# Gate steps reordered around the ReLU, and the gated activation written over it in one ring of four

## Chip, cores and metric

The kernel runs on one core of a Trainium2 chip. The metric is the device time of one execution, in microseconds (us); lower is better. Three executions of the kernel before gave a median of 2806.07 us.

## What is computed

A long convolution with a gate, then two wide two-matmul layers, all in float32. The part that matters here is the gate and the two layers behind it:

```python
y = np.fft.irfft(Uf * Hf[None, :, :], n=L, axis=1)[:, :S, :]
x = (x * y).reshape(B * S, D)          # the gate; B*S = 24960 tokens, D = 128
h = x @ w_in                           # 2048 hidden columns
x = (h * np.clip(h + 3.0, 0.0, 6.0) / 6.0) @ w_out
h = np.maximum(x @ w_in2, 0.0)
out = (h * h) @ w_out2
```

## The kernel before, in words

The first 465 us or so make the convolution's spectrum. The rest, the expert stage, is what the change touches. Its tokens come in 64 groups `j` of 390 (one `s4(j)` gives one group of the convolution's result) and are worked on in 49 tiles `t`: the first of 390 tokens, the others of up to 512. A tile can take tokens of one group or two; a group that lies across two tiles is rounded in two pieces.

The order of the work is written out by hand: `tiles` is a list of (layer, tile), and each entry has eight steps, of 256 hidden columns each. The first 15 tiles of layer 0 stand alone (early tiles); from then on tiles of layer 0 and of layer 1 alternate (the interleaved part), and at the end layer 1 is alone. Within a step `n`, the instructions are issued in this order, and each engine runs its own in the order issued:

- `l1(n)`: six matmuls into a PSUM tile `ph` (a ring of three), from the rounded input and its remainder. Matmuls need both as float32r: `oh`/`ol` in layer 0, `xh`/`xl` in layer 1 (high part, low part).
- `l2(n-3)`: six matmuls into the tile's sum `acc`. The first two need only the high part `gh` of an activation with the low weights, the last two the low part `gl`.
- `early_do[n]`: what the plan puts ahead of the ReLU.
- `relu(n)` on ScalarE into `r` (L618 in layer 0, L620 in layer 1), then `act(n)` on VectorE, which multiplies `r` with `ph` into `g` (L629, L632).
- `split(n-1)`: `gh` on ScalarE (L639, rounding), then `gl = g - gh` (L643), on VectorE or on GpSimd by the step's place in its tile. From step 112 on, even places are VectorE's, odd ones GpSimd's.
- `late_do[n]`: what the plan puts behind that, among it `combine(j)` (L500, sums of spectra for `s4`) and loads.
- one or two pieces of the decoding of the other weights (L104 to L127), whose last piece runs at 807.6 us.

`r` and `g` are rings of two each, so `act(n)` waits until `gl(n-2)` has read the `g` that it overwrites.

The gate of a group `j`: `s4(j)` is spread over a step or more between the matmuls of `l1` and `l2` and writes PSUM tile `py` (L517). VectorE multiplies it with the loaded `xt` in place (L532), ScalarE rounds it to `oh` (L534), VectorE subtracts to `ol` (L540). `py` lies in one of two banks that it shares with the sums `acc`: the bank is handed on to a tile's `acc` only when `ol` is done. For a tile that needs two groups, the first group's `s4` runs in the first one or two steps `8i`, `8i+1` of the tile before it in the list, and its bank is that of this tile's own `acc`, whose first matmul stands at step `8i+3`. On an early tile (`rate` 2) the product is planned at `8i+1` and `ol` at `8i+2`, in the interleaved part (`rate` 1) both at `8i+2`.

Of the kernel before, what the change touches and what calls it, by code (L numbers as in the profile page):

```python
# [7 lines left out]
F32 = mybir.dt.float32  # L8
F32R = mybir.dt.float32r
U32 = mybir.dt.uint32  # L10
AF = mybir.ActivationFunctionType
ALU = mybir.AluOpType
# [19 lines left out]
TM = 512  # L32
# [11 lines left out]
def tile_hyena_moe(ctx: ExitStack, tc, xg, vg, xT, pos, w1d, w2d, fmat, fwin, twc,  # L44
                   tws, twcf, twsf, dcs, inv, vtab, w_in1, w_out1, w_in2, w_out2, out):
    nc = tc.nc
# [234 lines left out]
    with tc.tile_pool(name="mlp", bufs=2, side="right") as mp, \  # L281
# [40 lines left out]
        for c in range(16):  # L322
# [10 lines left out]
            for q in range(4):  # L333
                ov = hs[q][:N1].rearrange("p d (h a) -> p a h d", h=2)
                src = fps[:N1, :, :, 32 * q:32 * q + 32]
# [32 lines left out]
    def idle(ps, count):  # L368
        for _ in range(count):
            nc.tensor.matmul(ps[:, 0, :TOK], wh[0][:, 0, :128], wh[0][:, 0, :TOK])  # L370
# [4 lines left out]
    with tc.tile_pool(name="cv_ps", bufs=4, space=PSUM) as vps:  # L375
# [17 lines left out]
        for i in range(NI + 2):  # L393
# [25 lines left out]
            for t, f in ((a + 6, load), (a + 3, product)):  # L419
                g, s = divmod(t, 3)  # L420
# [24 lines left out]
    mo = ctx.enter_context(tc.tile_pool(name="moe", bufs=2))  # L445
# [3 lines left out]
    def inputs(t):  # L449
        if (0, t) not in xin:  # L450
            xin[(0, t)] = tuple(mo.tile([128, TM], F32R, name=f"o{p}{t}", tag=f"o{p}", bufs=3)
                                for p in "hl")
        return xin[(0, t)]
# [50 lines left out]
    py = {}  # L504
# [19 lines left out]
    def ranges(j):  # L524
        for t in range(NTI):
            lo, hi = max(TOK * j, begins[t]), min(TOK * j + TOK, ends[t])
            if lo < hi:
                yield t, slice(lo - TOK * j, hi - TOK * j), slice(lo - begins[t], hi - begins[t])

    def gate(j):  # L530
        ps = py[j]
        nc.vector.tensor_tensor(ps[:, :TOK], ps[:, :TOK], xt.pop(j), ALU.mult)  # L532
        for t, src, dst in ranges(j):
            nc.scalar.activation(inputs(t)[0][:, dst], ps[:, src], AF.Copy)  # L534

    def gate_rest(j):
        ps = py.pop(j)
        for t, src, dst in ranges(j):
            h, l = xin[(0, t)]
            nc.vector.tensor_tensor(l[:, dst], ps[:, src], h[:, dst].bitcast(F32),  # L540
                                    ALU.subtract)

    begun, early_do, late_do = {}, {}, {}

    def plan(table, n, f, *args):
        table.setdefault(n, []).append((f, args))
# [7 lines left out]
    for t in range(1, NTI):  # L554
        js = list(range(last[t - 1] + 1, last[t] + 1))
        i = place_of[(0, t - 1)]
        n0, fast = NP * i, place_of[(0, t)] == i + 1
        if t == 1:
            jobs = [(js[0], 2, 2, i + 1), (js[1], 4, 2, i + 1)]
        else:  # L560
            jobs = [(js[-1], 4, 2 if fast else 0, i + 1)]
            if len(js) > 1:
                jobs.insert(0, (js[0], 0, 2 if fast else 1, i))
        assert len(js) == len(jobs)
        for j, q, rate, k in jobs:
            n = n0 + q
            plan(begun, n, s4, j, k)
            begun[n][-1] += (rate,)
            done = n + (4, 2, 1)[rate]
            gated[j] = done  # L570
            plan(early_do, done, gate, j)
            plan(early_do, done + (rate != 1), gate_rest, j)
            if j < 3:
                lead = (2, 1)
            elif j < 4:
                lead = (6, 5)
            else:
                lead = (7, 5)
            for back in lead:
                plan(late_do, n - back, combining, j)  # L580
            if j == 3:
                plan(late_do, 0, loads, j)
            elif j > 3:
                plan(late_do, gated[j - 3] + 1, loads, j)
# [12 lines left out]
    ph, rs, gs, gh, acc = ({} for _ in range(5))  # L597
# [15 lines left out]

    def relu(n):
        w = size[steps[n][1]]
        r = mo.tile([128, 2, TM], F32, name=f"r{n}", tag="r", bufs=2)
        if steps[n][0] == 0:
            nc.scalar.activation(r[:, :, :w], ph[n][:, :, :w], AF.Relu, bias=three)  # L618
        else:
            nc.scalar.activation(r[:, :, :w], ph[n][:, :, :w], AF.Relu)  # L620
        rs[n] = r

    def act(n):
        w = size[steps[n][1]]
        r, pv = rs.pop(n)[:, :, :w], ph.pop(n)[:, :, :w]
        gt = mo.tile([128, 2, TM], F32, name=f"g{n}", tag="g", bufs=2)
        g = gt[:, :, :w]
        if steps[n][0] == 0:
            nc.vector.scalar_tensor_tensor(g, r, 6.0, pv, ALU.min, ALU.mult)  # L629
        else:  # L630

            nc.vector.scalar_tensor_tensor(g, pv, 0.0, r, ALU.max, ALU.mult)  # L632
        gs[n] = g

    def split(n):
# [64 lines left out]
    decode(2, 1)  # L700
    decode(0, 3)
    gate(0)
    gate_rest(0)
    idle(mps.tile([128, 2, 512], F32, name="idle1", tag="ph", bufs=3), 6)
    decode(1, 3)
    decode(2, 6)
# [14 lines left out]
    for n in range(len(steps) + LAG + 1):  # L721
        if n < len(steps):
            l, j, q = steps[n]
            l1(n)
        m = n - LAG
        if 0 <= m < len(steps):
            l2(m)
        if 0 <= m - 1 < len(steps) and steps[m - 1][2] == NP - 1:
            finish(*steps[m - 1][:2])
        for f, args in early_do.pop(n, ()):  # L730
            f(*args)
        if n < len(steps):
            if q == 6 and n + 2 < len(steps) and steps[n + 2][0] == 1:
                part1(steps[n + 2][1])
            relu(n)
            act(n)
        if 0 <= n - 1 < len(steps):
            split(n - 1)
        for f, args in late_do.pop(n, ()):
            f(*args)  # L740
        for _ in range(2 if n < 14 else 1):
            next(rest, None)
# [94 lines left out]
```

## Time and profile before

| | before |
|---|---|
| median of three runs | 2806.07 us (2804.76 to 2806.34) |
| profiled execution, its own time | 2803.87 us |
| its span, first to last instruction | 2801.7 us |
| TensorE matmul (PE) busy | 2742.1 us, 98% |
| VectorE (DVE) busy | 1994.6 us, 71% |
| ScalarE (ACT) busy | 1931.6 us, 69% |
| GpSimd (POOL) busy | 1508.3 us, 54% |

Busy time is the time in which an engine has an instruction running. PE is the engine that has almost none to spare over the whole span; what the others do matters only where PE waits for them. The granted clock is the share of TensorE's full 2.4 GHz that it was given in a stretch: 0.5 is its lower level of 1.2 GHz. An idle time in a row is that of the engine just before the instruction, with what ended it.

### The profile page before, as it was taken

How to read it: one execution, taken by the hardware profiler on the slowest of the kernel's cores; microseconds unless marked ns; L12 is line 12 of the kernel's file. 1: busy time of each engine (PE TensorE's matmuls, PEld its weight loads, DVE VectorE, ACT ScalarE, POOL GpSimd, SP SyncE). 2: the span in 40 equal slices, each digit the busy share in tenths (PEclk: the TensorE clock that was granted, in tenths of full speed). 3: DMA queues.
4: the chain of work that ended last, by engine and by line, in shares of the span. 5: the costliest groups of instructions: out<-in, count | busy, mean ns of one | idle time of the engine just before them, and what ended most of it. 6: DMA issues, size and time to landing. Idle time of an engine off the chain costs nothing.

```text
span 2801.7 us, 34821 instructions
## 1 busy us (share of the span) xinstructions
PE 2742.1 (98%) x12862; PEld 2282.0 (81%) x12862; DVE 1994.6 (71%) x1976; ACT 1931.6 (69%) x2192; POOL 1508.3 (54%) x884
## 2 busy tenths in 40 slices
PE   7999998999999999999999999999999999999999
PEld 5899997777778888888888888888888888888887
DVE  6899998887876666666666666666666666666666
ACT  5445545666667777777777777777777777777776
POOL 3888884466565454444444444444545454444444
PEclk9999999999999999999999999999999999999999
DMA  3253535212111001010101010010101010000000
GB/s 120 85 165 109 149 112 123 79 31 71 40 32 34 25 18 35 18 35 18 35 18 35 19 35 19 25 29 25 29 25 29 25 29 4 8 8 12 12 12 16
DMA packets 136472, 122.35 MB, mean 44 GB/s; under 512 B 99370, under 2 KB 114798, under 8 KB 134894
## 3 DMA queue, kind: packets, MB, share of 16 engines
q1 hardware_dynamic: 127570, 86.27, 11.3%
q10 hardware_dynamic: 8732, 33.85, 4.4%
q8 instruction: 101, 1.65, 0.2%
q14 instruction: 69, 0.57, 0.1%
HBM read 83.68 MB, written 36.37 MB: 43 GB/s over the span
## 4 chain that ended last, share of the span: by engine, by line
PE 85%; DVE 6%; issue 3%; POOL 1%; ACT 1%; DMA 0%; POOLq 0%; DVEq 0%; ACTq 0%
PE acc L660 35%; PE ph L610 35%; PE p L225 7%; PE p L179 4%; PE py L517 3%; PE p L256 2%; DVE g L629 2%; DVE gl L643 1%; POOL gl L643 1%; ACT r L618 1%; ACT gh L639 0%; DVE wp L127 0%; DVE wa L114 0%; DVE py L532 0%; DVE a L198 0%
## 5 line engine op out<-in xcount | busy, mean ns | idle before, releaser
L643 POOL TENSOR_TENSOR gl<-g,gh 128x1024 fp32r<-128x1024 f32 (+2 forms) x401 | 970.7, 2421 | 1152.6 <-ACT gh L639 1101.0
L660 PE MATMUL acc<-gh,wp 128*128 128x512 f32 (+2 forms) x3136 | 878.7, 400 | 10.0 <-DVE ol L540 10.0
L639 ACT ACTIVATE gh<-g 128x1024 fp32r<-128x1024 f32 (+2 forms) x784 | 823.8, 1051 | 62.5 <-DVE g L629 36.2
L632 DVE SCALAR_TENSOR_TENSOR g<-ph,r 128x1024 f32<-128x1024 f32 (+2 forms) x392 | 477.9, 1219 | 363.6 <-POOL gl L643 268.1
L629 DVE SCALAR_TENSOR_TENSOR g<-r,ph 128x1024 f32<-128x1024 f32 (+2 forms) x392 | 475.9, 1214 | 361.9 <-POOL gl L643 276.5
L660 PEld LDWEIGHTS acc<-gh,wp 128*128 128x128 f32 x3136 | 577.9, 189 | 126.0 <-ACT gh L639 4.6
L618 ACT ACTIVATE r<-ph,three 128x1024 f32<-128x1024 f32 (+2 forms) x392 | 436.2, 1113 | 237.0 <-PE ph L610 232.4
L610 PE MATMUL ph<-oh,wp 128*128 128x512 f32 (+2 forms) x1568 | 573.3, 402 | 0.1
L610 PE MATMUL ph<-xh,wp 128*128 128x512 f32 (+2 forms) x1568 | 552.2, 393 | 0.0
L620 ACT ACTIVATE r<-ph 128x1024 f32<-128x1024 f32 (+2 forms) x392 | 401.8, 1025 | 177.2 <-PE ph L610 176.8
L660 PE MATMUL acc<-gl,wp 128*128 128x512 f32 (+2 forms) x1568 | 494.1, 396 | 8.6 <-POOL gl L643 8.1
L643 DVE TENSOR_TENSOR gl<-g,gh 128x1024 fp32r<-128x1024 f32 (+1 forms) x383 | 473.7, 1237 | 0.0
L660 PEld LDWEIGHTS acc<-gl,wp 128*128 128x128 f32 x1568 | 293.8, 189 | 83.3 <-POOL gl L643 14.8
L610 PEld LDWEIGHTS ph<-xh,wp 128*128 128x128 f32 x1568 | 294.4, 188 | 64.2
L610 PEld LDWEIGHTS ph<-oh,wp 128*128 128x128 f32 x1568 | 296.9, 189 | 59.6 <-ACT oh L534 0.4
L610 PE MATMUL ph<-ol,wp 128*128 128x512 f32 (+2 forms) x784 | 309.4, 395 | 4.0 <-DVE ol L540 4.0
L610 PE MATMUL ph<-xl,wp 128*128 128x512 f32 (+2 forms) x784 | 306.4, 391 | 0.0
L210 ACT ACTIVATE h<-a 128x720 fp32r<-128x720 f32 x96 | 77.3, 806 | 193.8 <-DVE a L198 163.5
L211 POOL TENSOR_TENSOR l<-a,h 128x720 fp32r<-128x720 f32 x96 | 167.7, 1747 | 63.7 <-ACT h L210 63.7
L610 PEld LDWEIGHTS ph<-ol,wp 128*128 128x128 f32 x784 | 148.5, 189 | 32.3 <-DVE ol L540 6.4
L610 PEld LDWEIGHTS ph<-xl,wp 128*128 128x128 f32 x784 | 147.4, 188 | 32.1
L534 ACT ACTIVATE oh<-py 128x390 fp32r<-128x390 f32 (+47 forms) x111 | 34.7, 357 | 152.0 <-DVE py L532 152.0
(97 smaller groups left out, 2699.2 us busy)
## 6 DMA issues: line engine op xcount, KB each, us to landing
zdb<-stg ACTq DMA_DIRECT2D x14, 1350.0 KB
x<-xg SPq DMA_DIRECT2D x64, 196.0 KB
v<-vg SPq DMA_DIRECT2D x64, 196.0 KB
xt<-xT SPq DMA_DIRECT2D x63, 195.0 KB
out<-ot ACTq DMA_DIRECT2D x47, 256.0 KB
za<-zdb SPq DMA_DIRECT2D x60, 180.0 KB
zb<-zdb SPq DMA_DIRECT2D x60, 180.0 KB
vt<-vtab SPq DMA_DIRECT2D x63, 137.8 KB
```

Of the source, the lines that this page charges most:

```text
L179: nc.tensor.matmul(ps[:, c // 2, o:o + 2 * K1], src, fm if s else fw)
L211: nc.gpsimd.tensor_tensor(l, gt, h.bitcast(F32), ALU.subtract)
L225: nc.tensor.matmul(pv, wt, x, start=(n == 0), stop=(n == len(ops) - 1))
L517: nc.tensor.matmul(ps[:, o:o + n], pm[j][q][:, r, b, :], v[:, q, r, :n], start=(r == 0), stop=(r == 1))
L610: nc.tensor.matmul(ps[:, c, :w], wt, x[:, :w], start=(m == 0), stop=(m == 2))
L618: nc.scalar.activation(r[:, :, :w], ph[n][:, :, :w], AF.Relu, bias=three)
L620: nc.scalar.activation(r[:, :, :w], ph[n][:, :, :w], AF.Relu)
L629: nc.vector.scalar_tensor_tensor(g, r, 6.0, pv, ALU.min, ALU.mult)
L632: nc.vector.scalar_tensor_tensor(g, pv, 0.0, r, ALU.max, ALU.mult)
L639: nc.scalar.activation(h, g, AF.Copy)
L643: eng.tensor_tensor(l, g, h.bitcast(F32), ALU.subtract)
L660: nc.tensor.matmul(ps, wt, x, start=(q == 0 and m == 0), stop=(q == NP - 1 and m == len(ops) - 1))
```

## The change

Three things are done. The gate's rounding to `oh` moves on ScalarE from ahead of the step's ReLU to behind `split(n-1)`, the end of the step. The subtraction to `ol` stays at the head of the step after the product, except in the interleaved part's two-group tiles (`rate` 1): there it moves from ahead of `act(n)` to the end of the same step. `act` writes its product over the ReLU's tile, so `r` and `g` become one ring of four tiles in the same memory. At the first tile, the `s4` of the second of its two groups begins one step later.

```diff
@@ def gate
     def gate(j):
         ps = py[j]
         nc.vector.tensor_tensor(ps[:, :TOK], ps[:, :TOK], xt.pop(j), ALU.mult)
+
+    def gate_high(j):
         for t, src, dst in ranges(j):
-            nc.scalar.activation(inputs(t)[0][:, dst], ps[:, src], AF.Copy)
-
-    def gate_rest(j):
+            nc.scalar.activation(inputs(t)[0][:, dst], py[j][:, src], AF.Copy)
+
+    def gate_low(j):
         ps = py.pop(j)
@@ the plan
-            jobs = [(js[0], 2, 2, i + 1), (js[1], 4, 2, i + 1)]
+            jobs = [(js[0], 2, 2, i + 1), (js[1], 5, 2, i + 1)]
@@
             plan(early_do, done, gate, j)
-            plan(early_do, done + (rate != 1), gate_rest, j)
+            plan(late_do, done, gate_high, j)
+            if rate == 1:
+                plan(late_do, done, gate_low, j)
+            else:
+                plan(early_do, done + 1, gate_low, j)
@@ relu and act
-        r = mo.tile([128, 2, TM], F32, name=f"r{n}", tag="r", bufs=2)
+        r = mo.tile([128, 2, TM], F32, name=f"r{n}", tag="r", bufs=4)
@@
-        r, pv = rs.pop(n)[:, :, :w], ph.pop(n)[:, :, :w]
-        gt = mo.tile([128, 2, TM], F32, name=f"g{n}", tag="g", bufs=2)
-        g = gt[:, :, :w]
+        g, pv = rs.pop(n)[:, :, :w], ph.pop(n)[:, :, :w]
         if steps[n][0] == 0:
-            nc.vector.scalar_tensor_tensor(g, r, 6.0, pv, ALU.min, ALU.mult)
+            nc.vector.scalar_tensor_tensor(g, g, 6.0, pv, ALU.min, ALU.mult)
         else:
-            nc.vector.scalar_tensor_tensor(g, pv, 0.0, r, ALU.max, ALU.mult)
+            nc.vector.scalar_tensor_tensor(g, pv, 0.0, g, ALU.max, ALU.mult)
```

What this does to the order of an engine is shown at three places; a name's number is its buffer's, and line numbers shift by up to six. First ScalarE at the gate of an early tile (the product is at 725.9 us in the trace), before:

```order
L618 ACTIVATE r_6390<-ph_6368,three 128x1024
L639 ACTIVATE gh_6394<-g_6359 128x1024
L534 ACTIVATE oh_6296<-py_6372 128x390
L618 ACTIVATE r_6414<-ph_6399,three 128x1024
L639 ACTIVATE gh_6418<-g_6392 128x1024
L618 ACTIVATE r_6437<-ph_6423,three 128x1024
```

and with the change:

```order
L624 ACTIVATE r_6318<-ph_6296,three 128x1024
L643 ACTIVATE gh_6321<-r_6286 128x1024
L624 ACTIVATE r_6340<-ph_6326,three 128x1024
L643 ACTIVATE gh_6343<-r_6318 128x1024
L536 ACTIVATE oh_6234<-py_6300 128x390
L624 ACTIVATE r_6363<-ph_6349,three 128x1024
```

The rounding that stood ahead of a ReLU and a `gh` now stands behind them; the same holds at every gate in the loop. The second place is VectorE at a gate of one piece in the interleaved part (the product is at 1511.7 us), before:

```order
L643 TENSOR_TENSOR gl_12887<-g_12859,gh_12886 128x1024
L532 TENSOR_TENSOR py_12843<-py_12843,xt_11939 128x390
L540 TENSOR_TENSOR ol_12657<-py_12843,oh_12656 128x390
L629 SCALAR_TENSOR_TENSOR g_12908<-r_12906,ph_12890 128x1024
L629 SCALAR_TENSOR_TENSOR g_12933<-r_12931,ph_12914 128x1024
```

and with the change:

```order
L647 TENSOR_TENSOR gl_12549<-r_12521,gh_12548 128x1024
L532 TENSOR_TENSOR py_12507<-py_12507,xt_11641 128x390
L633 SCALAR_TENSOR_TENSOR r_12566<-r_12566,ph_12552 128x1024
L542 TENSOR_TENSOR ol_12336<-py_12507,oh_12335 128x390
L633 SCALAR_TENSOR_TENSOR r_12592<-r_12592,ph_12575 128x1024
```

Here `ol` has moved behind the step's `act`. On ScalarE the rounding moves there as at the first place. The third place is TensorE at the start of the stage, from the last matmul of `l1(4)`'s first half on: `py_4493` is the second group's tile, `ph_4489` that of step 4, before:

```order
L610 MATMUL ph_4489<-oh_4321,wp_85 128x390
L517 MATMUL py_4493<-vt_4333,pp_4449 128x98 x2
L610 MATMUL ph_4489<-oh_4321,wp_85 128x390
L610 MATMUL ph_4489<-ol_4322,wp_85 128x390
L610 MATMUL ph_4489<-oh_4321,wp_85 128x390
L517 MATMUL py_4493<-vt_4333,pp_4449 128x98 x2
L660 MATMUL acc_0_4466<-gh_4445,wp_4191 128x390 x3
```

and with the change (`ph_4483` is step 4's tile, `ph_4516` step 5's, `py_4520` the second group's):

```order
L616 MATMUL ph_4483<-oh_4321,wp_85 128x390 x2
L616 MATMUL ph_4483<-ol_4322,wp_85 128x390
L616 MATMUL ph_4483<-oh_4321,wp_85 128x390
L664 MATMUL acc_0_4459<-gh_4442,wp_4191 128x390 x4
L664 MATMUL acc_0_4459<-gl_4443,wp_4191 128x390 x2
L616 MATMUL ph_4516<-oh_4321,wp_85 128x390
L616 MATMUL ph_4516<-ol_4322,wp_85 128x390
L616 MATMUL ph_4516<-oh_4321,wp_85 128x390
L517 MATMUL py_4520<-vt_4333,pp_4477 128x98 x2
```

The rest of `l1(4)`, all of `l2(1)` and half of `l1(5)` now stand ahead of the second group's first matmul. Its `combine` moves one step later on VectorE with it, and so do its product, rounding and subtraction.

## Rows read from the trace of the kernel before

**Rows 1.** Stretches: us, PE, PEld, DVE, ACT, POOL busy, granted clock, DMA share, GB/s.
```profile
475.00:498.00 23.00, 15.86 (x67) 14.98 (x68) 17.61 (x30) 9.12 (x14) 1.54 (x2) 0.70 0.91 220
...
526.00:535.00 9.00, 5.23 (x16) 3.91 (x17) 8.86 (x9) 3.37 (x5) 5.47 (x5) 0.81 0.00 0
...
568.00:575.00 7.00, 4.24 (x13) 3.09 (x12) 6.48 (x6) 6.27 (x8) 3.04 (x2) 0.76 0.32 79
575.00:727.50 152.50, 147.51 (x694) 119.20 (x694) 124.64 (x114) 105.36 (x121) 98.93 (x61) 1.00 0.18 48
727.50:735.00 7.50, 4.12 (x12) 3.01 (x11) 6.18 (x7) 6.34 (x8) 3.46 (x2) 0.77 0.31 74
...
811.00:815.00 4.00, 1.33 (x7) 0.81 (x6) 3.54 (x4) 4.00 (x6) 0.67 (x1) 1.00 0.56 138
...
900.00:2600.00 1700.00, 1700.00 (x7705) 1395.48 (x7704) 1120.34 (x1036) 1254.33 (x1358) 819.49 (x457) 1.00 0.09 23
```

**Rows 2.** Waits of PE, 480 to 900 us: us in total, times, longest.
```profile
PE acc L660 <- DVE ol L540: 10.0, 4, 3.4
PE acc L660 <- POOL gl L643: 7.3, 12, 1.0
PE py L517 <- issue: 4.6, 1, 4.6
PE ph L610 <- DVE ol L540: 3.8, 1, 3.8
```

**Rows 3.** Waits of ScalarE and VectorE, 480 to 900 us.
```profile
ACT oh L534 <- DVE py L532: 60.4, 20, 4.5
...
DVE g L629 <- POOL gl L643: 40.3, 25, 2.6
```

**Rows 4.** Timeline, start of the expert stage: start us, us, what, idle before.
```profile
485.81 0.36 PE L610 MATMUL ph<-oh,wp 128*128 128x390 f32 x1
...
486.31 0.97 DVE L629 SCALAR_TENSOR_TENSOR g<-r,ph 128x780 f32<-128x780 f32 x1 [1.36 <-ACT r L618]
...
490.07 0.56 DVE L540 TENSOR_TENSOR ol<-py,oh 128x390 fp32r<-128x390 f32 x1
490.73 1.14 PE L517 MATMUL py<-vt,pp 90*128 90x98 f32 x4 [4.57 <-issue]
```

**Rows 5.** Timeline, one wait on GpSimd.
```profile
606.77 0.56 ACT L534 ACTIVATE oh<-py 128x220 fp32r<-128x220 f32 x2 [3.54 <-DVE py L532]
...
609.36 2.39 POOL L643 TENSOR_TENSOR gl<-g,gh 128x1024 fp32r<-128x1024 f32 x1 [6.10 <-ACT gh L639]
```

**Rows 6.** Timeline, one gate of an early tile.
```profile
728.09 1.22 DVE L629 SCALAR_TENSOR_TENSOR g<-r,ph 128x1024 f32<-128x1024 f32 x1 [1.64 <-ACT r L618]
...
730.97 0.56 DVE L540 TENSOR_TENSOR ol<-py,oh 128x390 fp32r<-128x390 f32 x1
...
731.67 2.05 PE L660 MATMUL acc<-gh,wp 128*128 128x512 f32 x4 [3.38 <-DVE ol L540]
```

**Rows 7.** L117 in all of the run: ns least, median, most.
```profile
L117 DVE TENSOR_SCALAR wm<-wa x12: 405/1488/3815, 23.6 to 793.3; 128x512 uint32<-128x512 uint32 x12
```

**Rows 8.** Timeline, a gate of one piece in the interleaved part.
```profile
1511.21 0.40 PE L610 MATMUL ph<-oh,wp 128*128 128x512 f32 x1
...
1512.34 0.50 ACT L534 ACTIVATE oh<-py 128x390 fp32r<-128x390 f32 x1 [2.03 <-DVE py L532]
...
1512.73 1.11 ACT L618 ACTIVATE r<-ph,three 128x1024 f32<-128x1024 f32 x1
...
1512.87 0.56 DVE L540 TENSOR_TENSOR ol<-py,oh 128x390 fp32r<-128x390 f32 x1 [0.56 <-ACT oh L534]
...
1513.73 1.06 ACT L639 ACTIVATE gh<-g 128x1024 fp32r<-128x1024 f32 x1
...
1514.22 1.09 PE L660 MATMUL acc<-gh,wp 128*128 128x512 f32 x4
```

**Rows 9.** Groups by shape, ScalarE, 900 to 2300 us: count | busy, mean ns | idle.
```profile
L534 ACT ACTIVATE oh<-py 128x390 fp32r<-128x390 f32 x10 | 5.0, 498 | 20.3 <-DVE py L532 20.3
```

More of the change, by code (lines that the diff above doesn't have):

```diff
@@ L702, in tile_hyena_moe @@
     gate(0)
-    gate_rest(0)
+    gate_high(0)
+    gate_low(0)
     idle(mps.tile([128, 2, 512], F32, name="idle1", tag="ph", bufs=3), 6)
```

## The prediction

> **What bounds the kernel now.** I read PE's busy time by stretches first, to see where it is short of its stretch; a change off PE can only gain there. From 900 to 2600 us PE is busy in all 1700 us, at full clock [rows 1]. Nothing is to be had in that part: a wait removed on another engine there is worth nothing, and a wait added on PE costs its full length. Ahead of it there are holes: 7.1 us in 475 to 498 (23.00 less 15.86), 3.8 in 526 to 535, 2.8 in 568 to 575, 5.0 in 575 to 727.5, 3.4 in 727.5 to 735, 2.7 in 811 to 815. The granted clock shows a second cost. It is 0.70 in the first of these, 0.81, 0.76 and 0.77 in the three that follow a hole of 2.8 to 3.8 us, and 1.00 in the long one. Such a hole is mostly followed by a piece at 1.2 GHz: 0.19 x 9, 0.24 x 7 and 0.23 x 7.5 us are 1.7 us lost each.
>
> The list of PE's waits says what ended the holes [rows 2]. Four waits of `acc`, 10.0 us together, and one of `ph`, 3.8 us, were for `ol`, the gate's last step. Twelve, 7.3 us, were for GpSimd's `gl`. One of 4.6 us, of `py`, has no releaser named. The waits of the other engines over the same stretch tell what was late [rows 3]: ScalarE stood 60.4 us in front of `oh` until VectorE had done the product, 20 times, and VectorE stood 40.3 us in front of `act` until GpSimd's `gl` of two steps ago had freed a `g`.
>
> **The change, part by part.** The profiled execution took 2803.87 us, 2.2 below the median of the runs; I sum against 2803.87 and put the same difference on the median.
>
> *The start.* PE stopped at 485.81 in the middle of `l1(4)` and went on at 490.73 [rows 4]. What stood next is the second group's `s4`, whose bank the first group's `ol` had to free: it ended at 490.07 + 0.56 = 490.63, 0.1 us earlier. With the change `l1(4)`'s rest, `l2(1)` and half of `l1(5)` stand ahead, so they fill this hole. `ol` itself also comes earlier. `act(3)` at 486.31 had stood idle 1.36 us until its ReLU ended, which had been held behind `oh`; without that the same VectorE work, one half `combine` exchanged for another, ends 1.36 us earlier, at 489.3. So PE waits until about 489.4 instead of 490.7 (1.3 us), has three matmuls of `l1(4)`, six of `l2(1)` and three of `l1(5)` behind it, and should escape the second piece at 1.2 GHz. The twelve are 2.2 us, if a matmul of 390 columns takes 0.18 (an estimate: the row's 0.36 with an overlap of half). The escaped half clock is worth perhaps 2.7: 0.70 over 23 us is 13.8 us at half clock, I give this hole 5.4 of them, and half of that is lost. That is 6.2. VectorE then becomes the limit, since its order up to the second group's `ol` holds the same work, and that `ol` now stands one step ahead of `l1(8)`, which reads it, instead of two. I take off 2: the start gains 4, between 1 (the wait only moves) and 6.
>
> *The gate's rounding behind the ReLU, early tiles.* At one such gate `act` ran at 728.09 after 1.64 us of idleness, waiting for a ReLU that had stood behind `oh`; `ol` followed at 730.97 and PE, ready 3.38 us before, at 731.67 [rows 6]. I take it that the ReLU's matmuls were done, for the wait of `oh` is put down to the product, not to PE [rows 3]. With the ReLU ahead of `oh`, `act` follows the product at once, 1.64 us earlier, and so does `ol`, for `oh` fits under the `gl` between. That is the sure part: 1.64 at each of the five waits for `ol`, but 1.2 at one that was no longer (10.0 less 3.4, 2.8 and 2.7 [rows 1, 2]), 7.7 us. VectorE also comes to the gate itself earlier, since the gate before and the freed `g` waits let it catch up; I reckon a second 1.6 us for the longer ones, but not for all, because VectorE is still slowed there. So of 13.8 us some 10 go, and with them two of the three pieces at 1.2 GHz, 3.4: 13.4. Bounds are 7.7 and 18.9 (all of 13.8, and 3 x 1.7).
>
> *GpSimd's `gl`, early tiles.* At 606.77 `oh` ran after ScalarE had stood idle 3.54 us for the product; ReLU, `gh` and GpSimd's `gl` at 609.36 came behind it [rows 5]. With the ReLU and `gh` ahead of `oh`, up to 3.5 us of lateness leaves this chain, against PE waits for `gl` of at most 1.0 [rows 2]. Of the 7.3 us I take 5.5, since some have another `gl` or a `combine` in front on GpSimd; bounds 3 and 7.3.
>
> *The ring of four.* It removes `act`'s wait for `gl(n-2)`, counted in the terms above, and adds one of `relu(n)` for `gl(n-4)`. That one is met always: `l2(n-4)`, which reads `gl(n-4)`, stands ahead of `l1(n)` on PE, and `relu(n)` needs `l1(n)`. Writing over an input keeps the count and shape of the instructions; I cost it at nothing. What would hide a slower one is that VectorE is idle a third of the interleaved part (1120 of 1700 busy [rows 1]); ahead of 820 us it would come back in the terms above.
>
> *VectorE against GpSimd.* The row of L117 shows how work between SBUF tiles is stretched: 0.4 us at best, 1.5 in the median, 3.8 at most [rows 7]. The Trainium skill (SBUF — State Buffer, section "SBUF: two separate sides") states that VectorE's instructions that read two SBUF inputs or run in a two-port mode, and GpSimd's, take one port pair by an exclusive lock, and that the one that comes later waits for the whole instruction of the other. The trace agrees as far as L117's spread goes; no row tells its mode. By that rule the removed waits speak against this change, for they kept VectorE's `gl` and GpSimd's apart; this is a rival below.
>
> *The price: `ol` behind `act` in the interleaved part.* Here PE has no slack to hide anything beyond what the gate has now. `l1(8i+2)`'s last matmul ended at 1511.21 + 0.40 = 1511.61. `oh` ran at 1512.34, the ReLU at 1512.73, `ol` from 1512.87 to 1513.43, and the tile's first `acc` matmul at 1514.22, with no wait; from `ol` to PE takes 0.14 us where PE waits (731.53 to 731.67 [rows 6]), so the slack is 1514.22 - 1513.57 = 0.65 us [rows 8]. With the change the ReLU runs from about 1511.7 to 1512.8 and `gh` from 1512.7 to 1513.8 (1.11 and 1.06 us, each starting 0.1 before the end of the one ahead, as in the rows), `oh` from 1513.7 to 1514.2; `act` (1.22) ends near 1514.1, so `ol` goes by `oh`: 1514.25 to 1514.8, PE at 1514.95. That is 0.73 us of wait behind PE's `acc`, and behind it stands all that PE has. There are ten such gates: `oh` of one piece of 390 from 900 to 2300 us has a count of 10 [rows 9]; the other groups have their bank to themselves for some steps after `ol`. So 7.3 us are lost, between 3 (0.3 each, if the ReLU starts sooner or steps overlap more) and 11 (1.1 each, if `act` holds `ol` longer). The wait of 1.2 us, in 575 to 727.5, left the clock at 1.00 [rows 1], so I add none for the clock.
>
> *Sum.* 4 + 13.4 + 5.5 - 7.3 = 15.6 us gained: 2788.3 for a profiled execution, 2790.5 for the median.
>
> **The rivals.**
>
> A: the price is not paid, because the ten gates' `ol` still comes in time. It needs 0.73 us that I can't find in the rows; ScalarE is at most 0.1 us quicker between two instructions. The gains alone: 2806.1 - 22.9 = 2783.2.
>
> B: ahead of 820 us VectorE's own work is the limit, stretched by GpSimd, and not the waits. For it: from 526 to 535 VectorE is busy 8.86 of 9.00 us [rows 1]. Then work let go earlier only meets the port earlier, and holes come back a step later. The start's 4 and 3 of the `gl` waits remain against the price: 2806.1 - 7 + 7.3 = 2806.4. Against it: the 1.64 idle in rows 6 and the 3.54 in rows 5 lie right in the chains that end PE's holes.
>
> C, slower: in the interleaved part VectorE's `gl`, no longer held with its `act`, runs into GpSimd's, and a `gl` on GpSimd that starts up to 1.2 us later, with a `combine` of about the same length behind or ahead, makes PE wait step after step. With every second step late by 0.1 us, about 300 of some 600 steps there (7705 matmuls [rows 1], twelve a step and those of `s4`), 30 us would be lost: 2806.1 - 22.9 + 7.3 + 30 = 2820.5. It decides from 15.6 + 5.6 = 21 us, 0.07 us a late step. Against it: PE waits nowhere there now, and GpSimd is busy only 819 of 1700 us [rows 1].
>
> **How the numbers follow.** My forecast has 0.70, A 0.10, B 0.14, C 0.06. A difference of 0.2%, 5.6 us, is what a measurement of this kernel can tell from none. The forecast with all bounds the good way gives 6 + 18.9 + 7.3 - 3 = 29 us, all the bad way 1 + 7.7 + 3 - 11 = 1 us gained; both at once are unlikely, so it lies in 2778 to 2802 nine times in ten. That range holds A too, and leaves out B and C: 0.63 + 0.10, and some of the mild cases of B, near 0.77. Faster takes the forecast but for 0.04, A and little of B: 0.79. Same takes most of B and 0.04: 0.15. Slower is C: 0.06.
>
> **What would show it.** Right: no wait of PE's `py` near 490; one piece at half clock fewer at the start; waits of `acc` for `ol` of about 1 us in place of 2.7 to 3.4 on early tiles; waits for GpSimd's `gl` mostly gone by 820 us; no wait of `oh` for the product, of `act` for `gl`; and, new, ten waits of `acc` for `ol` of about 0.7 us from 905 to 2262. Wrong: holes of 3 us still at 530, 570 and 730 (B), PE waits for `gl` behind 900 (C), or no waits at the ten gates (A).

## The result

The changed kernel took 2780.66 us (median of 4 runs, 2779.70 to 2781.44), the kernel before 2805.41 us beside it: ratio 0.9912, interval 0.9895 to 0.9930, so 24.75 us faster. 2790.5 was predicted, in a range of 2778 to 2802. The profiled execution took 2781.44 us with a span of 2779.5, against 2803.87 and 2801.7: 22.4 us less, 22.2 of the span.

First the stretches of the profile after, in the columns of [rows 1].

```profile
475.00:498.00 23.00, 18.77 (x96) 17.90 (x96) 22.64 (x37) 14.42 (x21) 1.86 (x2) 0.85 0.96 240
526.00:535.00 9.00, 9.00 (x35) 7.21 (x34) 9.00 (x8) 7.16 (x8) 4.24 (x3) 0.85 0.01 2
568.00:575.00 7.00, 7.00 (x32) 5.68 (x31) 6.83 (x8) 5.60 (x8) 3.27 (x3) 1.00 0.43 101
575.00:727.50 152.50, 151.49 (x719) 124.87 (x719) 134.33 (x122) 114.82 (x131) 107.45 (x66) 1.00 0.19 52
880.00:2580.00 1700.00, 1695.41 (x7669) 1388.93 (x7669) 1118.63 (x1032) 1247.79 (x1353) 893.28 (x455) 1.00 0.09 23
```

PE is busy in all of 526 to 535 and 568 to 575, where it had stood for 3.8 and 2.8 us, and the second of these stretches has the full clock, where it had 0.76. In the long part at the end PE, which had no hole, now has 4.6 us of them. The waits, in the form of [rows 2, 3], say the same by cause. PE's over 480 to 880 us:

```profile
PE ph L616 <- DVE ol L542: 3.6, 2, 2.3
PE acc L664 <- DVE ol L542: 1.8, 2, 1.0
PE py L517 <- issue: 1.1, 1, 1.1
PE acc L664 <- POOL gl L647: 0.3, 1, 0.3
```

Those of VectorE and ScalarE over the same stretch:

```profile
DVE r L633 <- ACT r L624: 50.8, 44, 2.1
...
ACT oh L536 <- DVE py L532: 2.3, 4, 0.8
```

ScalarE's 60.4 us in front of `oh` are 2.3, VectorE's 40.3 us in front of `act` for GpSimd are gone from the list, and of PE's waits for `ol`, 13.8 us, 4.6 are left, 1.3 of them at a new place (0.8 of the 5.4 in the list are the first of the ten gates, at 878 us); of its 7.3 us for `gl`, 0.3.

To see where the time came from I set the same work side by side: from the last matmul ahead of step 11's ReLU to the ReLU of step 140, the early tiles behind the start (the ends agree to 0.2 us). Before, and after:

```profile
511.65:933.20 421.55, 400.46 (x1871) 326.65 (x1870) 328.19 (x302) 291.95 (x337) 252.24 (x154) 0.99 0.16 40
```

```profile
507.50:905.00 397.50, 392.99 (x1872) 326.37 (x1872) 333.71 (x303) 293.99 (x337) 259.36 (x154) 1.00 0.17 42
```

These steps became 24.05 us shorter. PE's holes went from 21.09 to 4.51 us, which is 16.6 (17.4 without the gate at 878 us); the other 7.5 us are in PE's "busy" column, for the same number of matmuls but one. The lead (start of the n-th ReLU before, less that after) tells the same by place: -0.6 us at step 0, 4.1 at step 8, 29.3 at step 132, the last ahead of the ten gates; then it falls by 0.95 at the first of these and by 0.75 at each of the others, to 21.6 at the last step. The changed kernel's second profiled execution (`e5_after_again`) began the stage 2.5 us earlier than before instead of 0.6 later, but its parts are nearly the same: 5.7 us from step 0 to 8 (4.7 here), 25.2 from there to step 132 (25.1) and 7.7 lost behind it (7.7). So leads are compared from step 0 on.

### The profile page after: what moved, and what is told of

The parts are those of the page before. It is cut to its first block, busy times and chain, and to the rows that moved or that the text cites. A ratio compares the mean times of both kernels' runs of the same rounds, so it can differ in the third digit from the quotient of the medians.

```text
span 2779.5 us, 33774 instructions
## 1 busy us (share of the span) xinstructions
PE 2736.8 (98%) x12862; PEld 2281.2 (82%) x12862; DVE 2000.7 (72%) x1976; ACT 1931.8 (70%) x2192; POOL 1594.1 (57%) x884
## 4 chain that ended last, share of the span: by engine, by line
PE 91%; DVE 3%; ACT 1%; issue 1%; DMA 0%; POOL 0%; POOLq 0%; SPq 0%; ACTq 0%; DVEq 0%
PE acc L664 37%; PE ph L616 37%; PE p L225 7%; PE p L179 4%; PE py L517 4%; PE p L256 2%; DVE r L633 1%; ACT gh L643 0%; ACT r L624 0%; DMA za<-zdb 0%; DVE ol L542 0%; DVE gl L647 0%; DVE wm L117 0%; DVE wa L125 0%; DVE wa L114 0%
## 5 line engine op out<-in xcount | busy, mean ns | idle before, releaser
L647 POOL TENSOR_TENSOR gl<-r,gh 128x1024 fp32r<-128x1024 f32 (+2 forms) x401 | 966.9, 2411 | 1045.3 <-ACT gh L643 990.4
L643 ACT ACTIVATE gh<-r 128x1024 fp32r<-128x1024 f32 (+2 forms) x784 | 820.0, 1046 | 17.9 <-DVE r L633 17.5
L633 DVE SCALAR_TENSOR_TENSOR r<-r,ph 128x1024 f32<-128x1024 f32 (+2 forms) x392 | 475.4, 1213 | 355.0 <-ACT r L624 351.6
L636 DVE SCALAR_TENSOR_TENSOR r<-ph,r 128x1024 f32<-128x1024 f32 (+2 forms) x392 | 478.0, 1219 | 339.9 <-ACT r L626 339.7
L664 PEld LDWEIGHTS acc<-gh,wp 128*128 128x128 f32 x3136 | 575.6, 188 | 124.6 <-PE ph L616 10.8
L647 DVE TENSOR_TENSOR gl<-r,gh 128x1024 fp32r<-128x1024 f32 (+1 forms) x383 | 473.6, 1237 | 0.0
L500 POOL TENSOR_TENSOR pp<-za,zb 90x256 f32<-90x256 f32 x122 | 134.7, 1125 | 37.3 <-ACT gh L643 37.3
```

What stands on the lines that cost most here:

```text
L500: eng.tensor_tensor((p, n)[k][:, :, r], za[:, :, r], zb[:, :, 1 - r], (ALU.add, ALU.subtract)[k])
L633: nc.vector.scalar_tensor_tensor(g, g, 6.0, pv, ALU.min, ALU.mult)
L636: nc.vector.scalar_tensor_tensor(g, pv, 0.0, g, ALU.max, ALU.mult)
L643: nc.scalar.activation(h, g, AF.Copy)
L647: eng.tensor_tensor(l, g, h.bitcast(F32), ALU.subtract)
L664: nc.tensor.matmul(ps, wt, x, start=(q == 0 and m == 0), stop=(q == NP - 1 and m == len(ops) - 1))
```

## The experiments

Two theories stood against each other. **W**: the ReLU was held behind the gate's rounding, which waited for the product; the new order of the gate is what pays. **R**: VectorE was held at `act` until GpSimd's `gl` had freed a tile; the ring of four is what pays. Beside them stood what is left: the price at the ten gates, and the early waits that stayed, which rival B of the prediction would put down to VectorE's stretched work. All medians are beside runs of the kernel before on the same chip, in three groups of runs (before: 2803.99, 2805.53 and 2805.51 us).

**The ring alone** (`e1_ring`). Kernel before, and:

```diff
-        r = mo.tile([128, 2, TM], F32, name=f"r{n}", tag="r", bufs=2)
+        r = mo.tile([128, 2, TM], F32, name=f"r{n}", tag="r", bufs=4)
...
-        gt = mo.tile([128, 2, TM], F32, name=f"g{n}", tag="g", bufs=2)
...
-            nc.vector.scalar_tensor_tensor(g, r, 6.0, pv, ALU.min, ALU.mult)
+            nc.vector.scalar_tensor_tensor(g, g, 6.0, pv, ALU.min, ALU.mult)
...
```

> Only the ring of four with the product written over the ReLU's tile; the gate and the start as before. Theory W (the ReLU held behind the gate's rounding is what made TensorE wait; the ring matters little): 2 to 5 us faster than before, the waits of act for gl(n-2) gone but the waits of acc for ol still near 2 to 3 us. Rival R (VectorE held at act by GpSimd's gl is what made it late): 13 to 18 us faster, with most of the waits for ol gone.

Measured: 2805.72 us, ratio 1.0006 (0.9997 to 1.0015). Waits from 480 to 900 us of PE, then of VectorE and ScalarE:

```profile
PE acc L658 <- POOL gl L641: 7.3, 10, 1.3
PE acc L658 <- DVE ol L540: 6.0, 2, 3.3
PE acc L658 <- ACT gh L637: 5.6, 3, 3.7
```

```profile
DVE r L627 <- ACT r L618: 71.0, 51, 3.7
...
ACT oh L534 <- DVE py L532: 61.1, 20, 6.5
```

VectorE no longer waits for GpSimd, but waits for the ReLU instead, since ScalarE still stands 61.1 us in front of `oh`. The wait that the ring removes was not the last one; R falls as the main cause. The 2 to 5 us that W gave the ring did not come either.

**The gate's order alone** (`e2_gate`). Kernel before, with two rings of two and the start unchanged:

```diff
+    def gate_high(j):
         for t, src, dst in ranges(j):
...
-            plan(early_do, done + (rate != 1), gate_rest, j)
+            plan(late_do, done, gate_high, j)
+            if rate == 1:
+                plan(late_do, done, gate_low, j)
+            else:
+                plan(early_do, done + 1, gate_low, j)
```

> Only the gate's order (rounding behind the ReLU, subtraction at the next step's head, behind act at the ten gates); two rings of two and the start as before. Theory W: 13 to 19 us faster than before, the ten gates' price of 6 to 8 us in it. Rival R: 0 to 5 us faster, waits for ol only about 1.6 us shorter each.

Measured: 2783.52 us, ratio 0.9930 (0.9917 to 0.9942), 20.5 us faster. VectorE's largest group of waits over 480 to 900 us is the old one:

```profile
DVE g L635 <- POOL gl L649: 46.2, 28, 2.5
```

It is more than the 40.3 us of before, and PE loses next to nothing by it: its waits for `gl` are 1.1 us in all of the run. W holds: nearly all of the gain is here, and a little more than the 13 to 19 us that were expected of it.

**The start alone** (`e3_start`): `jobs = [(js[0], 2, 2, i + 1), (js[1], 5, 2, i + 1)]` in place of 4.

> Only the second group's s4 one step later at the first tile; gate and rings as before. Both theories: 3 to 5 us faster, the wait of py at 490 us 1.2 to 3 us in place of 4.6. If it is below 1 us, the start's gain in the changed kernel came from the gate's order and not from this.

Measured: 2802.49 us, ratio 0.9997 (0.9988 to 1.0006), less than the 3 to 5 us expected and not told from none by the time. In the trace PE's wait of `py` there is 2.6 us instead of 4.6:

```profile
PE py L517 <- issue: 2.6, 1, 2.6
```

The lead, 0.65 us already at step 0, is 3.2 at step 8 and 2.9 at the end, so this change alone is worth 2.2 to 2.5 us. The gate's order alone has 0.9 by step 8 (`e2_gate`); the 4.7 of the changed kernel's start need both.

**The ten gates in the old order** (`e4_old_at_ten`, and once more as `e10_old_at_ten_again`). Changed kernel, and:

```diff
-            plan(late_do, done, gate_high, j)
             if rate == 1:
-                plan(late_do, done, gate_low, j)
+                plan(early_do, done, gate_high, j)
+                plan(early_do, done, gate_low, j)
             else:
+                plan(late_do, done, gate_high, j)
                 plan(early_do, done + 1, gate_low, j)
```

> The changed kernel, but at the ten gates of the interleaved part (rate 1) product, rounding and subtraction stand at the head of the step in the old order. If the order there is the whole price: 6 to 9 us faster than the changed kernel, 30 to 33 us faster than before, no wait of acc for ol behind 870 us. If the waits there have another cause (the ring, the bank), the time stays that of the changed kernel.

> The kernel with the old order at the ten gates and the ring, once more, beside the one without the ring and with less decoding: 29 to 33 us faster than before; with less decoding and no ring it should be 4 to 9 us faster than this, of which the decoding is 3 to 5.

Measured: 2773.83 us, ratio 0.9893 (0.9880 to 0.9907), and 2772.87, ratio 0.9880 (0.9864 to 0.9897). PE has no hole in the interleaved part:

```profile
880.00:2580.00 1700.00, 1700.00 (x7699) 1395.06 (x7699) 1122.79 (x1036) 1254.21 (x1361) 900.65 (x458) 1.00 0.09 23
```

The lead is that of the changed kernel up to step 132 (29.2 us) and stays there. So the ten waits are the price of the late rounding and subtraction at these gates, 7.7 us by the lead, and nothing is got for it.

**The changed kernel again** (`e5_after_again`), to stand beside the next three.

> The changed kernel once more, beside the three below: 23 to 27 us faster than before.

Measured: 2778.78 us, ratio 0.9911 (0.9897 to 0.9925), 26.8 us faster than before, as expected.

**The rounding ahead of `gh`** (`e6_before_gh`). As `e4_old_at_ten`, but at all gates other than the ten `oh` stands between the ReLU and the `gh` that follows it:

```diff
             relu(n)
+            for f, args in mid_do.pop(n, ()):
+                f(*args)
             act(n)
...
-                plan(late_do, done, gate_high, j)
+                plan(mid_do, done, gate_high, j)
```

> Old order at the ten gates; at all other gates the rounding stands behind the ReLU but ahead of act and of gh(n-1). Theory W in two parts (the ReLU ahead of the rounding ends the waits for ol, gh ahead of it those for GpSimd's gl): 4 to 8 us slower than the same kernel with the rounding at the step's end, which was 30 us faster than before; waits of acc for ol stay short, waits for gl come back to 4 to 7 us. Rival (only the ReLU's place counts): within 1.5 us of it.

Measured: 2783.03 us, ratio 0.9921 (0.9907 to 0.9936): 22.5 us faster than before, where the kernel that it is an edit of was 30.2 and 32.6 faster. So most of the gain comes already with the ReLU alone ahead of the rounding. ScalarE waits for the product again, and PE, over 480 to 2700 us, for more than one thing:

```profile
ACT oh L536 <- DVE py L532: 17.0, 14, 3.4
```

```profile
PE acc L665 <- ACT wp L123: 3.0, 1, 3.0
PE acc L665 <- DVE ol L542: 2.8, 2, 2.4
...
PE acc L665 <- POOL gl L648: 1.5, 4, 0.7
```

That `gh` also has to stand ahead of the rounding is shown by the time: 8 to 10 us. That the loss would come back as waits for `gl` was mostly wrong. Against `e4_old_at_ten` they rose from 0.3 to 1.5 us, and behind 505 us those for `ol` did not rise (2.8, there 3.3); the largest new wait is the 3.0 us put down to a decoded weight (L123), with a granted clock of 0.83 over 715 to 725 us. It ends the same chain on ScalarE:

```profile
713.89 0.50 ACT L536 ACTIVATE oh<-py 128x390 fp32r<-128x390 f32 x1 [3.44 <-DVE py L532]
...
717.17 0.63 ACT L123 ACTIVATE wp<-wa 128x512 fp32r<-128x512 f32 x1
...
717.81 1.76 PE L665 MATMUL acc<-gh,wp 128*128 128x512 f32 x4 [3.02 <-ACT wp L123]
```

`oh` had stood 3.44 us for the product; `gh`, a ReLU, another `gh` and L123 followed it without a break, and PE went on as L123 ended.

**Less decoding beside the first steps** (`e7_less_decode`). As `e4_old_at_ten`, with `2 if n < 12` in place of 14 in the loop that gives VectorE's weight decoding to the steps: steps 12 and 13 take one piece each instead of two, and all later pieces come two steps later.

> Old order at the ten gates, and one piece of decoding in place of two at steps 12 and 13, so that two VectorE instructions stretched to 2.9 and 3.9 us by GpSimd no longer both stand ahead of the group's subtraction. If VectorE's own stretched work is what is left of the early waits: the wait of ph for ol of 2.3 us goes below 0.5 with its piece at half clock, 3 to 4.5 us faster than with the old order at the ten gates alone, 33 to 35 us faster than before. If the hole only moves on: no faster.

Measured: 2768.03 us, ratio 0.9869 (0.9855 to 0.9883), 37.5 us faster than before, more than the 33 to 35 expected. All that PE waits for from 505 to 2700 us is

```profile
PE acc L665 <- POOL gl L648: 0.3, 1, 0.3
```

and around the place of the 2.3 us wait PE is busy throughout, at full clock:

```profile
520.00:535.00 15.00, 15.00 (x70) 11.98 (x68) 15.00 (x15) 11.53 (x13) 12.85 (x10) 1.00 0.00 1
```

So the wait of 2.3 us for `ol` that the changed kernel kept was due to decoding on VectorE: here rival B was right. The half-clock piece behind that wait is less regular. With the same 2.3 us wait the profiled executions of the changed kernel, of `e5_after_again` and of `e10_old_at_ten_again` have 0.89 over these 15 us, those of `e2_gate`, `e4_old_at_ten` and `e8_no_ring` 1.00. The changed kernel's line, then that of `e4_old_at_ten`:

```profile
520.00:535.00 15.00, 12.66 (x48) 9.88 (x47) 14.96 (x12) 8.52 (x10) 9.97 (x9) 0.89 0.02 4
```

```profile
520.00:535.00 15.00, 12.67 (x55) 9.95 (x54) 14.96 (x12) 9.04 (x10) 10.46 (x9) 1.00 0.05 11
```

**Without the ring** (`e8_no_ring`): `e4_old_at_ten` with two rings of two, the ReLU and `g` in tiles of their own, as before.

> Old order at the ten gates, and the two rings of two put back; gate order and start as changed. If the ring is worth nothing beside the gate's order: within 1 us of the same kernel with the ring (30 us faster than before). If the ring helps VectorE catch up once the ReLU is out of the way: 3 to 6 us slower than that, with waits of act for gl(n-2) back and waits for ol of more than 1 us at more than two early gates.

Measured: 2771.57 us, ratio 0.9882 (0.9868 to 0.9896), 34.0 us faster than before, where the two runs with the ring were 30.2 and 32.6. Beside the new order the ring is worth nothing either; whether the kernel is a little faster without it these runs don't settle.

**What the runs point to** (`e9_both`): `e8_no_ring` and `2 if n < 12` together.

> Everything that the runs so far point to: the gate's new order but the old one at the ten gates, the later start of the second group, one piece of decoding at steps 12 and 13, and the two rings of two. If the ring is worth nothing here either: 36 to 40 us faster than before. If the ring is needed once the decoding is out of the way: 33 us or less.

Measured: 2766.93 us, ratio 0.9861 (0.9846 to 0.9876), 38.6 us faster than before, as expected, and the lowest median here, though `e7_less_decode` (37.5 us faster) can't be told from it. The interleaved part:

```profile
880.00:2580.00 1700.00, 1700.00 (x7694) 1394.92 (x7693) 1125.03 (x1036) 1252.23 (x1360) 819.66 (x457) 1.00 0.09 23
```

## Why the prediction was right, and where its sum was off

**What bounds the kernel.** Right: all of the gain lies ahead of the first of the ten gates (878 us in the trace after), and the ten waits from there on cost their full length and more.

**The start** (+4, 1 to 6). Right: the lead rises by 4.7 us from step 0 to step 8. The timeline after:

```profile
485.06 0.96 DVE L633 SCALAR_TENSOR_TENSOR r<-r,ph 128x780 f32<-128x780 f32 x1
...
487.99 0.34 PE L616 MATMUL ph<-oh,wp 128*128 128x390 f32 x1
...
488.81 0.56 DVE L542 TENSOR_TENSOR ol<-py,oh 128x390 fp32r<-128x390 f32 x1
...
489.47 0.66 PE L517 MATMUL py<-vt,pp 90*128 90x98 f32 x4 [1.15 <-issue]
```

`act` comes 1.25 us earlier and `ol` 1.26 (1.36 was reckoned), and PE waits until 489.47; 489.4 was predicted. That this fits so well is in part luck, for the stage began 0.6 us later here than before, so against its own beginning `act` comes 1.85 us earlier. The clock over 475 to 498 us is 0.85 instead of 0.70, which is 3.4 us where 2.7 were reckoned. That VectorE becomes the limit behind it, for which 2 us came off, shows as one of the two waits of `ph` in the list: 1.27 us at 499.1, in front of `l1(8)`.

**The early tiles** (13.4 for `ol` and 5.5 for `gl`, 18.9 in all). Right in its mechanism: `e1_ring` and `e2_gate` put it on the ReLU behind `oh`. **This is the term that was mis-sized**: the equal work gives 24.05 us and 0.95 that the first of the ten gates took from it, 25.0 (25.1 by the lead) in place of 18.9, near the upper bounds of the two terms, 18.9 and 7.3. Of the holes I had counted 15.5 us as gone (10 of the 13.8 for `ol`, 5.5 of the 7.3 for `gl`), and 17.4 went: a smaller miss of 1.9. The larger one is in PE's busy column: I gave it 3.4, two half-clock pieces of three, and 7.5 went. The clock's part of that is as predicted. One piece is left: the stretch from 526 us on cuts it, but 0.89 over 520 to 535 us is 3.3 us at half clock, 1.7 lost, where three had cost 5.1, so 3.4 came back. What I left out altogether is what a hole costs beyond itself. At a gate below a hole of 0.51 us makes PE's next matmul start 0.67 late, since the matmuls around it no longer overlap. Some 14 holes fewer in the lists of waits by 0.16 would be 2.2 us more (an estimate); the last 1.9 of the 7.5 I cannot assign to a row.

**What stayed.** The prediction kept some wait for `ol` because VectorE is slowed beside GpSimd. One such wait is this, in the timeline after:

```profile
517.60 2.40 POOL L647 TENSOR_TENSOR gl<-r,gh 128x1024 fp32r<-128x1024 f32 x1 [5.04 <-ACT gh L643]
...
517.70 2.85 DVE L114 TENSOR_TENSOR wa<-wa,wg 128x512 f32<-128x512 f32 x1
...
519.95 1.90 POOL L500 TENSOR_TENSOR pp<-za,zb 90x256 f32<-90x256 f32 x2
...
520.58 3.87 DVE L117 TENSOR_SCALAR wm<-wa 128x512 uint32<-128x512 uint32 x1
...
521.81 2.35 POOL L647 TENSOR_TENSOR gl<-r,gh 128x1024 fp32r<-128x1024 f32 x1
...
524.37 0.61 DVE L542 TENSOR_TENSOR ol<-py,oh 128x244 fp32r<-128x244 f32 x2
...
524.82 0.50 PE L616 MATMUL ph<-ol,wp 128*128 128x512 f32 x1 [2.34 <-DVE ol L542]
```

L117, which takes 0.41 us at its best, took 3.87, from 520.58 to 524.45: through the rest of GpSimd's two `combine` and all of its `gl`, which ended at 524.16. `ol` stood behind it, and PE waited 2.34 us. With one piece of decoding less there (`e7_less_decode`) `ol` started at 519.94 and the wait was gone. The other early wait that stayed, 1.0 us at 711 us, is absent from the lists of `e8_no_ring` and of `e7_less_decode`; its cause stays open.

**The ring** (nothing, and no cost of writing in place). Right: layer 0's `act` takes 1213 ns in the mean of the whole run after (L633) and 1214 before (L629), and the ring alone moved the time by nothing. The ReLU's new wait was not quite always met in advance: one ReLU, at 543.6 us after, stood 2.1 us until GpSimd was done, but PE was busy all the while (33.0 of 33 us over 535 to 568).

**The price at the ten gates** (7.3, or 0.73 each). Right. One of them:

```profile
1485.14 0.40 PE L616 MATMUL ph<-oh,wp 128*128 128x512 f32 x1
...
1485.64 1.12 ACT L624 ACTIVATE r<-ph,three 128x1024 f32<-128x1024 f32 x1 [1.40 <-PE ph L616]
...
1486.65 1.05 ACT L643 ACTIVATE gh<-r 128x1024 fp32r<-128x1024 f32 x1
...
1487.60 0.48 ACT L536 ACTIVATE oh<-py 128x390 fp32r<-128x390 f32 x1
...
1487.93 0.39 PE L616 MATMUL ph<-oh,wp 128*128 128x512 f32 x1
...
1488.11 0.56 DVE L542 TENSOR_TENSOR ol<-py,oh 128x390 fp32r<-128x390 f32 x1
...
1488.82 1.17 PE L664 MATMUL acc<-gh,wp 128*128 128x512 f32 x4 [0.51 <-DVE ol L542]
```

The chain is the predicted one, ReLU, `gh`, `oh`, `ol`, 2.47 us from the ReLU to `ol` where 2.55 was reckoned. The hole is 0.51 us; from one matmul's start to the next PE lost 0.90 less the usual 0.23, or 0.67 us; the lead falls by 0.75, and by 7.7 over the ten. The prediction's 0.73 was such a delay of PE's start, so it is met; that the waits themselves would be about 0.7 us was too much. The clock stayed at 1.00.

**The rivals.** A is out: the price is paid, though A's 2783.2 is nearer to the measured 2780.66; the early tiles gained more than was forecast, which hid it. B is out as the main cause, since 17.4 of the 21.1 us of holes went; what `e7_less_decode` and `e9_both` gained beside the same kernel with more decoding, some 5 to 7 us, is its part. C's mechanism came, though not its price: with the ring GpSimd's busy time in 1700 us of the interleaved part rose from 819 to 893 us, but PE waited there for no `gl`.

The account of the profiled execution, with the signs of the sum: 4.7 (4) and 25.1 (18.9), less 7.7 (7.3), less 0.6 that the stage began later, is 21.5 us by the steps against 22.2 of the span.

## What to carry to other kernels

An instruction that waits long in an engine's queue costs what stands behind it, not itself: look at what is queued behind such a wait and who at the end waits for that, before freeing a buffer on another engine. Where two waits lie in one chain, as ScalarE's for the product and VectorE's for a free tile, taking away the earlier-ending one gives nothing. A new order that pays where the bounding engine has holes should be kept away from the places where it has none: here the same edit gained 25 us in one part and lost 7.7 in another, and one `if` by the gate's rate was enough to have the first without the second.

## What the runs showed of the hardware that was not expected

A hole on TensorE costs more than the list of waits says. The list counts from the end of the matmul before, 0.39 us after its start, while in a run the next matmul starts 0.23 us after it. So 0.51 us of idleness cost 0.67 from start to start, and the 17 holes of the kernel before from 511 to 900 us, 21.0 us of idleness, took 27.7 us from start to start, 0.16 each beyond the hole and the usual 0.23.

GpSimd's pair of small `combine` instructions (L500) takes 1.44 us when VectorE's `act`, which reads one of its inputs from PSUM, runs beside it, and about 1 us more when VectorE's `gl` does, which reads two tiles in SBUF. Before:

```profile
1503.19 1.44 POOL L500 TENSOR_TENSOR pn<-za,zb 90x256 f32<-90x256 f32 x2
1503.28 1.22 DVE L632 SCALAR_TENSOR_TENSOR g<-ph,r 128x1024 f32<-128x1024 f32 x1 [1.68 <-POOL gl L643]
```

and after:

```profile
1520.39 2.43 POOL L500 TENSOR_TENSOR pp<-za,zb 90x256 f32<-90x256 f32 x2
...
1520.95 1.27 DVE L647 TENSOR_TENSOR gl<-r,gh 128x1024 fp32r<-128x1024 f32 x1
```

VectorE's `gl` lost next to nothing (1.27 us for 1.22), GpSimd waited. By the groups of 900 to 2300 us the mean of one L500 went from 744 to 1226 ns, and that of its other half (`pn`) from 752 to 1234; over 880 to 2580 us both together went from 124.6 to 198.1 us, which makes up nearly all that GpSimd is busier. One half, before and after:

```profile
L500 POOL TENSOR_TENSOR pp<-za,zb 90x256 f32<-90x256 f32 x78 | 56.4, 744 | 0.0
```

```profile
L500 POOL TENSOR_TENSOR pp<-za,zb 90x256 f32<-90x256 f32 x78 | 93.8, 1226 | 0.0
```

It is the ring that does it: over 880 to 2580 us one half takes 1237 ns with the ring alone (`e1_ring`) and 754 with the gate's order alone (`e2_gate`), and kernels without the ring (`e9_both`: 819.66 us) have the old busy time. The likely link is the wait for GpSimd that the ring takes from VectorE, 435.7 us over that stretch before and none after. The Trainium skill (SBUF — State Buffer, section "SBUF: two separate sides") states that such instructions of the two engines exclude each other from a shared port pair for a whole instruction, and these rows agree with it. In the other direction it was dearer: the L117 above took 3.87 us instead of 0.41, through instructions of GpSimd that followed one another. The other seven L117 on `wm` behind it show the same. Three met no GpSimd instruction at their start and took 0.41 to 0.42 us, though a `gl` began 0.06 and 0.12 us behind two of them; four started while a `gl` ran and ended 0.28 or 0.29 us after its end, as the long one did.
